# Giving out PSUM by the bank, merging a pair of PE pieces, loading B ahead of x, and planning the kernel's order anew

## The chip, the cores and the metric

One core of one Trainium2 chip. The metric is the device time of one execution in microseconds (us). Every execution has a state: most agree well, some run at a lower granted TensorE clock and are called slow; only fast runs are compared. A "ratio" below is the mean time of one kernel's fast runs over the mean of the other's fast runs in the same rounds on the same chip, with a 95% interval; so it is not quite the ratio of the medians that are quoted beside it.

Medians and ranges in the tables and texts are those of all runs, slow ones included.

Engines: PE is TensorE (PEld its weight loads), DVE VectorE, ACT ScalarE, POOL GpSimd, SP SyncE; SPq and POOLq are the transfers that these issue. PSUM is the memory into which PE's matmuls write; the program uses eight banks of it, of 512 fp32 columns each. "L1105" is line 1105 of the kernel's source. The change moves lines: L1105 (output matmuls) becomes L1110, L1114 (DVE's read of an output) L1119, L877 (B products) L882, L891 (odd states) L889, L741 (stage 1) L747, L754 (spectrum) L760, L780 (inverse) L786, L799 (final) L805, L515 (PSUM copy) L520, L706 (POOL's add on ssm_k) L712, L959 (gates) L964.

## The reference, cut to what matters

```python
# x: 1 x 2048 x 1024, 1024 states, bf16
g = sigmoid((x * gate_w).sum(-1, keepdims=True))
# a: a diagonal state-space model: products with B, a scan over time, products with C
Bu = einsum("bld,pd->blp", x, B_bar)            # complex
h_t = Lam_bar * h_{t-1} + Bu_t
a = 2 * einsum("blp,dp->bld", hseq, C).real + x * Dskip
# b: a long convolution per channel, by Fourier transforms
kv = shift(k, shift_k) * v
b = x * (irfft(rfft(kv) * rfft(ssm_k)) + kv * ssm_D)
out = g * a + (1 - g) * b
```

## The kernel before: the parts that matter

The kernel does not issue its work in program order. It records operations with a duration, a priority and the tiles they use; a planner of its own then simulates the five engines and the buffers, picks a place for each tile, and emits all operations in the order of their planned start. From that order a recording layer underneath derives every semaphore wait. The planner's duties thus include PSUM:

```python
    psums = [psum.tile([128, 1024], F32, name=f"ps{i}") for i in range(4)]   # four allocations of two banks
    ...
    # in the planner: a PSUM tile takes one whole pair of banks, the one that has been free longest
    fr = [i for i in range(self.nps) if psf[i] is None]
    if not fr:
        break
    t.place = min(fr, key=lambda i: self.ps_last[i])
    psf[t.place] = t
```

The last stage makes 32 output tiles of 128x512, each by 16 matmuls and one DVE operation that reads PSUM. Two share one pair of banks:

```python
            ps = pl.psum([2, 512])
            def one(ti):
                def f():
                    for i, pi in enumerate(korder):
                        for ri in range(2):
                            PE_.matmul(ps.ap[:, ti, :], lhsT=Hr[...], rhs=CT[...], start=..., stop=...)
                op("PE", 16 * MM(512), f, r=[...], w=[(ps, ti)], prio=prs[ti])
                op("DVE", 0.77, lambda: STT(out=ot.ap[:, ti, :], in0=ps.ap[:, ti, :], scalar=col(gcols, gi[ti]),
                                            in1=pb.ap[:, ti, :], op0=ALU.mult, op1=ALU.add),
                   r=[(ps, ti), pb, e_gate], w=[(ot, ti)], prio=prs[ti])
            one(0)
            one(1)
```

The states of even steps need products with x (L877) and with the odd states (L891), which before are two PE operations on one PSUM tile. The convolution's kernel ssm_k comes in eight loads of 512 KB; the first is issued by POOL at 8.5 us, beside the first loads of B and x.

## Time and profile before

| | before |
|---|---|
| time, median (lowest to highest), 3 runs | 439.74 us (432.97 to 446.48) |
| profiled run: span, PE busy, DVE busy | 432.5 us, 93%, 80% |

Two groups of the profile before, with PE's output matmuls and DVE's read of them (columns: engine, operation, output and inputs, shapes, count; busy us, mean ns of one; idle us of the engine just before, and what ended it):

```profile
L1105 PE MATMUL ps<-slab,slab 128*128 128x512 bf16 x499 | 111.6, 379 | 2.9 <-DVE slab L1114 1.9
...
L1114 DVE SCALAR_TENSOR_TENSOR slab<-ps,gcols,slab 128x512 bf16<-128x512 f32 x32 | 23.4, 747 | 47.7 <-PE ps L1105 46.1
```

All 32 output tiles together cost PE 2.9 us of idle time. PE hardly ever waits for DVE here.

### The profile page before, as it was taken

Reading aid. Unit: us, or ns where it says so; the run is one execution under the profiler, and the core shown is the slowest. Engines: PE = TensorE matmul, PEld = TensorE weight load, DVE = VectorE, ACT = ScalarE, POOL = GpSimd, SP = SyncE. Lnnn points to the kernel's source line nnn. Section 1 sums busy time; section 2 is a strip of 40 time slices with the busy share of each in tenths; the row PEclk is TensorE's granted clock in tenths of the full one; section 3 lists DMA queues with packets and bytes.
Section 4 is the critical chain, followed back from the end, with each engine's and each line's share of the span. In section 5 each row is a group of like instructions: output and inputs, shape, how many; then the busy total and the mean of one; then the engine's idle time right before and its main releaser. Section 6 shows DMA issues by size and latency. Waiting matters only on the chain. (4 is left out here: it accounts for less than half of the span.)

```text
span 432.5 us, 7209 instructions
## 1 busy us (share of the span) xinstructions
PE 401.3 (93%) x2679; PEld 230.1 (53%) x2726; DVE 344.8 (80%) x509; ACT 282.0 (65%) x316; POOL 144.1 (33%) x190
## 2 busy tenths in 40 slices
PE   7398999999999899999999997998999989999996
PEld 7344545555467555555665654675555534444442
DVE  5974899999999889999999897996767667841542
ACT  3776676599788978986987897895636627211100
POOL 8920763135253565331374562222231200000000
PEclk9979999999999999999999999999999999999999
DMA  9999859946999999999739999997999834611411
GB/s 148 83 190 196 167 120 225 235 106 124 229 246 197 162 179 183 165 156 238 148 71 223 199 182 228 312 243 124 163 206 236 212 72 121 212 56 49 147 36 61
DMA packets 137531, 71.86 MB, mean 166 GB/s; under 512 B 113669, under 2 KB 130325, under 8 KB 137497
## 3 DMA queue, kind: packets, MB, share of 16 engines
q1 hardware_dynamic: 128328, 49.30, 61.8%
q0 software_dynamic: 9088, 22.10, 24.0%
q8 instruction: 21, 0.34, 0.4%
q14 instruction: 14, 0.11, 0.1%
q10 hardware_dynamic: 80, 0.01, 0.0%
HBM read 24.93 MB, written 16.79 MB: 96 GB/s over the span
## 5 line engine op out<-in xcount | busy, mean ns | idle before, releaser
L515 ACT CAST slab<-ps 128x1024 bf16<-128x1024 f32 x194 | 183.0, 1036 | 58.9 <-PE ps L782 13.9
L877 PE MATMUL ps<-slab,slab 128*128 128x512 bf16 (+1 forms) x529 | 115.3, 370 | 8.9 <-DMA slab<-in_A_B_re_dram 6.1
L1105 PE MATMUL ps<-slab,slab 128*128 128x512 bf16 x499 | 111.6, 379 | 2.9 <-DVE slab L1114 1.9
L877 PEld LDWEIGHTS <-slab 128*128 128x128 bf16 x544 | 53.1, 99 | 63.6 <-DMA slab<-in_A_B_re_dram 6.0
L510 POOL DMA_DIRECT2D slab<-slab x92 | 55.7, 611 | 87.7 <-ACT slab L515 78.7
L1105 PEld LDWEIGHTS <-slab 128*128 128x128 bf16 x512 | 49.8, 98 | 60.7 <-issue 2.6
L1114 DVE SCALAR_TENSOR_TENSOR slab<-ps,gcols,slab 128x512 bf16<-128x512 f32 x32 | 23.4, 747 | 47.7 <-PE ps L1105 46.1
L1087 ACT ACTIVATE slab<-slab,omgc 128x512 bf16<-128x512 bf16 x32 | 20.9, 718 | 40.9 <-DMA slab<-pB_scr 40.9
L754 PE MATMUL ps<-slab,fC 128*128 128x512 bf16 x115 | 43.5, 379 | 1.7 <-ACT slab L515 1.1
L906 DVE TENSOR_TENSOR slab<-slab,slab 128x2048 bf16<-128x2048 bf16 x29 | 35.4, 1221 | 7.3 <-ACT slab L515 5.3
L766 DVE TENSOR_TENSOR slab<-slab 128x2048 bf16<-128x2048 bf16 x32 | 38.4, 1215 | 1.2 <-ACT slab L515 1.2
L741 PE MATMUL ps<-tab,slab 128*128 128x128 bf16 x512 | 35.0, 220 | 4.0 <-ACT slab L515 4.0
L741 PEld LDWEIGHTS <-slab 128*128 128x128 bf16 x512 | 31.2, 98 | 8.6 <-issue 5.3
L755 PE MATMUL ps<-slab,fS 128*128 128x256 bf16 x128 | 34.8, 272 | 0.7
L756 PE MATMUL ps<-slab,fN 128*128 128x256 bf16 x128 | 34.9, 272 | 0.0
L780 PE MATMUL ps<-slab,gC 128*128 128x256 bf16 x128 | 29.9, 273 | 2.9 <-DVE slab L770 2.8
L782 PE MATMUL ps<-slab,gS 128*128 128x128 bf16 x128 | 28.0, 219 | 0.0
L781 PE MATMUL ps<-slab,gN 128*128 128x128 bf16 x128 | 28.0, 219 | 0.0
L729 DVE TENSOR_TENSOR slab<-slab,slab 128x2046 bf16<-128x2046 bf16 (+2 forms) x22 | 26.8, 1216 | 0.1
L770 DVE TENSOR_TENSOR slab<-slab 128x512 bf16<-128x512 bf16 x64 | 24.4, 417 | 0.5 <-PE ps L782 0.4
L727 ACT ACTIVATE slab<-slab,skc 128x2047 bf16<-128x2047 bf16 (+2 forms) x11 | 22.2, 2030 | 2.9 <-DMA slab<-in_B_k_dram 2.9
L802 DVE TENSOR_TENSOR slab<-ps,slab 128x1024 bf16<-128x1024 f32 x16 | 19.4, 1220 | 5.0 <-PE ps L800 4.2
(180 smaller groups left out, 553.7 us busy)
## 6 DMA issues: line engine op xcount, KB each, us to landing
slab<-slab POOLq DMA_DIRECT2D x92, 64.0 KB, 6.3
slab<-in_A_x_dram SPq DMA_DIRECT2D x20, 256.0 KB
slab<-kv_scr POOLq DMA_DIRECT2D x8, 512.0 KB, 7.4
slab<-pB_scr SPq DMA_DIRECT2D x16, 256.0 KB
slab<-h_scr SPq DMA_DIRECT2D x8, 512.0 KB
out_dram<-slab SPq DMA_DIRECT2D x15, 256.0 KB
slab<-in_A_x_dram POOLq DMA_DIRECT2D x11, 256.0 KB, 6.4
slab<-in_B_ssm_k_dram SPq DMA_DIRECT2D x5, 512.0 KB
```

Source lines behind the costliest of these rows:

```text
L510: QS[q].dma_start(out=o_, in_=i_)
L515: op("ACT", 1.04, lambda: A.copy(o_(), i_()), r=r, w=w, prio=prio, alt=("DVE", 1.2, lambda: V.tensor_copy(o_(), i_())))
L741: PE_.matmul(ps.ap[:, i, :], lhsT=a.ap[:, 8 * q + i, :], rhs=t1v[:, hh * 128:(hh + 1) * 128], start=True, stop=True)
L754: PE_.matmul(ps.ap[:, i], lhsT=fC[:, k2, :], rhs=zz, start=True, stop=False)
L755: PE_.matmul(ps.ap[:, i, :, 0, :], lhsT=fS[:, k2, :], rhs=zz[:, :, 1, :], start=False, stop=False)
L756: PE_.matmul(ps.ap[:, i, :, 1, :], lhsT=fN[:, k2, :], rhs=zz[:, :, 0, :], start=False, stop=True)
L766: TT(out=T.ap, in0=K.unsqueeze(2).to_broadcast([128, 2, 2, 4 * CH]), in1=W_.unsqueeze(1).to_broadcast([128, 2, 2, 4 * CH]), op=ALU.mult)
L780: PE_.matmul(ps.ap[:, i], lhsT=gC[:, k2, :], rhs=pp.ap[:, :, i, :], start=True, stop=False)
L781: PE_.matmul(ps.ap[:, i, 0, :], lhsT=gN[:, k2, :], rhs=pp.ap[:, 1, i, :], start=False, stop=False)
L877: PE_.matmul(ps.ap[:, ri, k0:k1], lhsT=BT.ap[:, d, ri, :], rhs=t.ap[:, d, k0:k1], start=(d == 0), stop=(par == 1 and d == ND - 1))
L906: TT(out=out, in0=tab.ap.unsqueeze(2).to_broadcast([128, 2, 2, CW]), in1=x.unsqueeze(1).to_broadcast([128, 2, 2, CW]), op=ALU.mult)
L1105: PE_.matmul(ps.ap[:, ti, :], lhsT=Hr[pi, a // 4].ap[:, par, ri, (a % 4) * 128:(a % 4 + 1) * 128], rhs=CT[pi, dh][0].ap[:, CT[pi, dh][1], ...
```

## The change

Intent: a 512-column output needs only one bank, so a bank is to come free as soon as its own tile is read; the even-state tile is to be held for a shorter time; the loads that PE needs first are to be alone on the DMA engines; and the planner's priorities and buffer counts were searched anew for this. Cut to its core (new priorities left out: they change every number of the tables):

```diff
     def psum(self, shape):
+        t.banks = 1 if n <= 512 else 2
...
-                    fr = [i for i in range(self.nps) if psf[i] is None]
+                    n = t.banks
+                    fr = [i for i in range(0, self.nps, n) if all(x is None for x in psf[i:i + n])]
-                    t.place = min(fr, key=lambda i: self.ps_last[i])
-                    psf[t.place] = t
+                    t.place = min(fr, key=lambda i: (n == 1 and psf[i ^ 1] is None, max(self.ps_last[i:i + n])))
+                    psf[t.place:t.place + n] = [t] * n
...
-                        a = psums[t.place]
+                        a = psums[t.place // 2][:, 512 * (t.place % 2):]
...
-    NSLAB, NPS = 21, 4
+    NSLAB, NPS = 21, 8
...
         def load_A(src, u, tag, ex, pr):
+            ex = ex + ([(xT[0, NC - 1], 1)] if u < 2 else [])     # not before the last x tile
...
-            (even states: part(0, CW) and the odd-state products as two PE operations)
+                op("PE", 2 * ND * MM(CW) + 4 * MM(511) + (0.2 if c else 0), lambda: (part(0, CW), prev()), ...)
...
-        BTs = [loadB(0, (-1000, -988.5)), loadB(1, (-986.5, -986))]
+        BTs = [loadB(0, (-1000, -999)), loadB(1, (-986.5, -986))]
...
-            ps = pl.psum([2, 512])
             def one(ti):
+                ps = pl.psum([512])
-                            PE_.matmul(ps.ap[:, ti, :], ...
+                            PE_.matmul(ps.ap, ...
```

## The prediction

> **What bounds the kernel now.** I read the page first (parts 1 and 2), then busy time by stretches, then PE's waits, then the instructions in order of time around each wait.
>
> ```profile
> span 432.5 us, 7209 instructions
> PE 401.3 (93%) x2679; PEld 230.1 (53%) x2726; DVE 344.8 (80%) x509; ACT 282.0 (65%) x316; POOL 144.1 (33%) x190
> ...
> PE   7398999999999899999999997998999989999996
> ...
> PEclk9979999999999999999999999999999999999999
> ```
>
> PE is the bound: 93% busy, and the thin slices lie at the start, about two thirds on, and around 355 us. No change of the diff removes a matmul, so the question is how much of the span is not needed by PE. I work PE's own need out from rows where it runs without a gap: the chain has 49 output matmuls of 512 columns (L1105) in 10.74 us, 0.219 us each. L1105 512, the B products L877 512 (in whole equivalents), L891 and L943/L945 64+32+64, L799/L800 64: 1248 x 0.219 = 273.6 us. The spectrum (L754 to L756) takes 0.435 us a step, x128 = 55.7; the inverse (L780 to L782) 0.89 us a piece of four steps, x32 = 28.5; stage 1 (L741) 0.45 us a piece, x64 = 28.6; gates and small ones some 3.5. Sum 390 us. So 432.5 - 390 = 42.5 us are lost, and only these can be won.
>
> ```profile
> 15.00:20.00 5.00, 1.42 (x14) 1.02 (x11) 4.85 (x20) 4.97 (x3) 4.91 (x4) 0.95 1.00 57
> 20.00:25.00 5.00, 2.43 (x6) 1.04 (x8) 4.82 (x8) 3.31 (x10) 3.88 (x4) 0.50 1.21 194
> ...
> 265.00:270.00 5.00, 2.22 (x13) 1.14 (x13) 2.31 (x3) 4.80 (x6) 1.28 (x5) 0.87 1.04 284
> ```
>
> The columns are PE, PEld, DVE, ACT, POOL busy, clock, DMA share, GB/s. Up to 46.3 us PE does only about 24.4 us of the needed work (96 B products 21.0, gates 2.0, the rest 1.4): **head loss 21.9 us**. After the last matmul (428.5 us) come 4.0 us of last DVE operation and store: **tail loss 4.0**. The rest, **16.6 us, is lost in the body**.
>
> ```profile
> 11.07 1.91 PE L877 MATMUL ps<-slab,slab 128*128 128x256 bf16 x16
> 14.52 1.91 PE L877 MATMUL ps<-slab,slab 128*128 128x256 bf16 x16 [1.54 <-DMA slab<-in_A_x_dram]
> 22.57 15.69 PE L877 MATMUL ps<-slab,slab 128*128 128x512 bf16 x78 [6.15 <-DMA slab<-in_A_B_re_dram]
> ```
>
> The largest single gap is 6.15 us at 22.57: PE has used x's first tile for state block 0 and waits for B of block 1. After it the clock is 0.50 until 26.4 us, another 1.9 us lost.
>
> ```profile
> PE ps L741 <- ACT slab L515: 4.0, 6, 2.7
> PE ps L780 <- DVE slab L770: 2.8, 3, 1.5
> PE ps L1105 <- DVE slab L1114: 1.9, 1, 1.9
> PE ps L754 <- ACT slab L515: 1.1, 4, 0.3
> ```
>
> (Total, times, longest.) Stage 1 reads only loaded data and constants, so its wait on ACT's PSUM copy is a wait for a free PSUM pair. With the same kind at L754, L943, L877, L891 and L1105, waits for a pair or for what was just copied come to some 7.4 us in the body; L780's are for DVE's product and no PSUM matter.
>
> **What the Trainium skill says.** "TensorE: Matmul & The Clock Gate", Part 1: an idle window of about 3.4 us brings the clock to half, and as much busy time restores it. The trace agrees: after the 6.15 us gap the clock is 0.50. At 267 us a gap of 2.67 us also cost clock (0.87), so shorter gaps are not safe. "DMA: Bandwidth & Descriptors", Issuing engines are not separate DMA queues: transfers from different engines interleave on the same 16 DMA engines. The trace agrees: the POOL queue issues a 512 KB load of ssm_k at 8.52 us, and B's 512 KB, issued at 8.91 and 10.26, land only at about 22.2, in a stretch that runs down to 57 GB/s. "PSUM — Partial Sum Buffer", the four PSUM rules: one matmul output is at most one bank, 512 fp32 columns. So a 512-column output tile needs just one bank; giving it two is the plan's grain, not the chip's need.
>
> **The change part by part.**
>
> *x before the convolution's loads, B ahead of x.* Loads of ssm_k and kv for the first two channel blocks, and the first x rows of the convolution, now wait for the last transposed x tile. B_im of block 0 moves ahead of x, but the first 16 matmuls need both B halves and the first x piece anyway, so that order is worth about 0. Taking ssm_k away is worth more. x's second half tile lands at 14.5. From 22.2 to 40.9 the six other x half tiles come at 18.7 / 6 = 3.1 us per 512 KB. At that rate B of block 1 lands at 14.5 + 3.1 = 17.6, say 18, not 22.2, and the last x at 36.7, not 40.9. PE and DVE both wait for x in the head (gates at 40.96, the first rotations after it), so the plan starts some **4.2 us earlier**; the gap shrinks to about 2 us and most of the 1.9 us of cold clock goes, though part of that only becomes waiting for x: **-0.5**. Moved to later: the 512 KB of ssm_k. Its first user, stage 1, is at 38.1 us, so it may now be late; PE has other blocks' B products then, so I take 0.
>
> *PSUM per bank.* Only the 32 output tiles (and the gates) are one bank; spectrum, stage 1, inverse, final and B products still take an aligned pair. So up to 291 us, where L1105 starts, it changes next to nothing. After it, an output pair was held until both halves had been read. Here is what that cost:
>
> ```profile
> 352.29 0.75 DVE L1114 SCALAR_TENSOR_TENSOR slab<-ps,gcols,slab 128x512 bf16<-128x512 f32 x1 [3.44 <-PE ps L1105]
> 355.07 0.75 DVE L1114 SCALAR_TENSOR_TENSOR slab<-ps,gcols,slab 128x512 bf16<-128x512 f32 x1
> 355.87 6.42 PE L1105 MATMUL ps<-slab,slab 128*128 128x512 bf16 x29 [1.90 <-DVE slab L1114]
> ```
>
> PE sat 1.90 us until DVE had read the second half at 355.07, since the other pairs held two final pieces. With banks the first half is free at 353: **-1.9**, and -0.3 for the wait at 291. From 362 to 428 outputs run without a gap already: nothing to win there.
>
> *Even products in one piece.* Before, a pair was taken at the x part and kept until the odd states were there: at 231.65 the x part ends, at 236.5 the four L891 start, 4.9 us with three pairs left for all else; elsewhere 0 to 3 us. 16 such pieces. No instruction is saved. The small waits of 0.2 to 0.5 us for a pair, in all about 4.4 us without the one of 2.67, have other causes too (ACT needs 1.02 us for a pair, a conv piece on PE 0.45 to 0.89), so I give this a quarter: **-1.1**.
>
> *Priorities and buffer counts.* This moves everything and removes nothing. What is left of the body's loss after the above is 16.6 - 3.3 = 13.3 us, among it 4.2 us around 267 (a 2.67 us wait and the clock after it): ACT stood behind a pB read that came late, which a plan does not foresee. A newly searched order may win some of that and meet new late transfers: **-1.5, give or take 4**.
>
> Sum: -4.2 - 0.5 - 2.2 - 1.1 - 1.5 = -9.5, span 423.0. The profiled run took 434.26 us for a span of 432.5, so 1.8 more: 424.8 in a quiet run. The three timed runs were 432.97, 439.74 and 446.48; the quiet one lies 1.3 below the profiled run and the middle one 5.5 above. I take 2 us of such scatter: **427 us**.
>
> **Rivals.** (a) *DVE becomes the bound of the body.* From 46 to 290 us DVE is busy 229.5 of 244 us (94%), PE 232.9 (95%). If the chain of rotations and scans on DVE sets when the outputs may start, a faster PE start is won only as far as DVE starts sooner too, and PSUM relief is worth nothing. For: DVE is at 4.9 to 5.0 of 5 us in most stretches. Against: DVE drops to 3.2 of 10 us from 30 to 40 while it waits for the first states, which come earlier too; and from 290 on it has room for convolution work. It would make -5 us: 430 quiet. (b) *The new plan runs into late transfers.* Loads put off in the head make ssm_k or kv late for stage 1, and ACT or PE, strictly in order, stand behind them, as at 267. Each such event costs 3 to 4 us with the clock; two of them leave 429 to 432. (c) *False ordering between two banks of one tile*: an output in one bank would wait for the reader of its neighbour. Against: before, PE wrote the second half while DVE read the first, without a gap for 66 us. Would cost 10 us or more; I give it 3%. (d) *The search does better*: DVE work moved behind 300 us, body loss halved, head as computed: -14, 418.5 quiet.
>
> **Range and chances.** Main path and its neighbours 423 to 429, (a) and (b) up to 434, (d) down to 418; scatter of some us: 418 to 436. The quiet run of before is 433 to 434, so 2% faster means below about 425, just where my quiet estimate lies; measured against the median before, 427 is 2.9% faster. Hence 0.54 faster, 0.43 within 2%, 0.03 slower.
>
> **What would show it.** Right: in the changed kernel PE's gap before block 1's B products is at most 3 us and ends by 19, the clock stays near 1.00 there, gates start by 37.5; no wait of L1105 on L1114 over 0.5 us; the L891 matmuls follow straight on their L877; PE busy falls only by 1 to 3 us, nearly all of the gain being idle time. Wrong: ssm_k was not what delayed B (the gap stays 5 us or more); PE's waits on the PSUM copy stay at 6 us or more; or new waits on transfers over 2 us between 50 and 360 us.

## The result, and the profile after

| | before | after |
|---|---|---|
| median (lowest to highest) of 6 runs each | 439.39 us (432.97 to 446.48) | 458.06 us (454.64 to 467.53) |
| ratio, fast runs | | 1.046, interval 1.034 to 1.058 |
| profiled run, both fast | 434.26 us | 457.16 us |

The change is 4.6% slower. Parts 1 and 2 of the page after (in the rows of part 2 each digit stands for a fortieth of the span and gives the busy share, or the granted clock, in tenths):

```profile
span 455.4 us, 7234 instructions
...
PE 405.7 (89%) x2679; PEld 231.4 (51%) x2726; DVE 346.6 (76%) x511; ACT 289.2 (64%) x315; POOL 148.0 (33%) x192
...
PE   7789999999899998999899887899699988787875
...
PEclk9999999999999999999999999899799999999999
```

The work is the same; PE is 89% busy and not 93%. Compare the ends of the two PE rows. Before, the last seven slices were 9s but for the final one; after, they are 8, 7, 8, 7, 8, 7, 5: PE loses a fifth of its time in the very stage that had nothing to lose. The first digits are better than before, and the clock in the head no longer drops. Stretches of the head after (columns as in the prediction):

```profile
15.00:20.00 5.00, 3.46 (x19) 1.77 (x20) 4.85 (x20) 4.54 (x3) 4.92 (x4) 1.00 1.10 210
20.00:25.00 5.00, 4.12 (x28) 2.41 (x26) 4.44 (x8) 4.08 (x10) 4.83 (x3) 1.00 1.08 180
```

PE in order of time in the head, after:

```profile
16.54 5.15 PE L882 MATMUL ps<-slab,slab 128*128 128x512 bf16 x31 [1.54 <-DMA slab<-in_A_B_re_dram]
...
22.57 8.87 PE L882 MATMUL ps<-slab,slab 128*128 128x512 bf16 x47 [0.88 <-DMA slab<-in_A_x_dram]
...
35.19 1.91 PE L964 MATMUL ps<-slab,gwb 128*32 128x512 bf16 x31 [2.57 <-DMA slab<-in_A_x_dram]
```

The 6.15 us wait for B is 1.54 us, and the bulk of the gates starts at 35.2, not 40.96. The head came out as meant. PE's waits (us in total, times, longest):

```profile
PE ps L1110 <- DVE slab L1119: 18.8, 21, 1.9
...
PE ps L747 <- POOL slab L712: 2.6, 1, 2.6
PE ps L786 <- ACT slab L520: 2.3, 4, 1.1
...
PE ps L747 <- ACT slab L520: 1.4, 4, 0.7
```

The first line is new: 21 times PE, about to start an output tile, waited for DVE's read of an output. The same in the groups of the page:

```profile
L1110 PE MATMUL ps<-slab,slab 128*128 128x512 bf16 x485 | 115.5, 386 | 19.5 <-DVE slab L1119 18.8
...
L1119 DVE SCALAR_TENSOR_TENSOR slab<-ps,gcols,slab 128x512 bf16<-128x512 f32 x32 | 23.8, 749 | 72.3 <-PE ps L1110 71.3
```

DVE's read is as long as before (749 ns), and DVE is idle 72 us ahead of these reads, so DVE is not overloaded: it waits for PE, and PE for it. How, shows in order of time, first PE, then DVE:

```profile
367.13 3.61 PE L1110 MATMUL ps<-slab,slab 128*128 128x512 bf16 x16 [0.84 <-DVE slab L1119]
371.58 3.61 PE L1110 MATMUL ps<-slab,slab 128*128 128x512 bf16 x16 [0.84 <-DVE slab L1119]
376.04 3.61 PE L1110 MATMUL ps<-slab,slab 128*128 128x512 bf16 x15 [0.84 <-DVE slab L1119]
```

```profile
370.78 0.75 DVE L1119 SCALAR_TENSOR_TENSOR slab<-ps,gcols,slab 128x512 bf16<-128x512 f32 x1 [1.78 <-PE ps L1110]
375.24 0.75 DVE L1119 SCALAR_TENSOR_TENSOR slab<-ps,gcols,slab 128x512 bf16<-128x512 f32 x1 [3.71 <-PE ps L1110]
```

A strict turn: a tile on PE (367.13 to 370.74), then DVE's read (370.78 to 371.53), then the next tile (371.58). One tile takes 4.45 us where its matmuls need 16 x 0.219 = 3.50 us. With eight banks to choose from, an output's matmuls and an output's read never run at the same time here.

The list of the built program's instructions, with their places and waits, says why (counts are those that each engine's semaphore has reached):

```
after                                             before
MM tile 30 -> ps1, bank 0   waits DVE 508         MM tile 25 -> ps1, bank 1   waits DVE 493
   ends: PE count 2710                            MM tile 26 -> ps1, bank 0   waits for nothing
   DVE reads tile 29, ps1 bank 1, waits PE 2710      ends: PE count 2646
   done: DVE count 509                               DVE reads tile 25, ps1 bank 1, waits PE 2646
MM tile 31 -> ps1, bank 1   waits DVE 509            DVE reads tile 26, ps1 bank 0
   ends: PE count 2726                            MM tile 27 -> ps3, bank 1   waits DVE 496
```

After: tile 29 is complete before tile 30 starts, but its reader waits for PE count 2710, the **end of tile 30, which goes to the other bank**. That wait is not needed by the data. Tile 31 then truly has to wait for this reader, as it gets tile 29's bank. So each read falls between two tiles. The wait exists because the recording layer orders by the whole allocation `ps1` of two banks. In the program before, the same unneeded wait is there (tile 25 is read only after the end of tile 26), but PE's next tile goes to another allocation and does not feel it. The new key sends outputs into the half next to a taken half, so from one point on all outputs alternate between the two banks of `ps1`.

To see where else time came and went, I followed PE's progress: each matmul's weight load counted with the duration that the prediction's rows give it, so that the total is 390 us. The table has the time at which a given amount of this work was begun, minus the same of before's profiled run (-5 is 5 us ahead). It depends on the durations taken, most of all at 105, and is to be read to some 2 us. It is used for all runs below.

| needed work begun (us) | 30 | 105 | 240 | 255 | 300 | 330 | end |
|---|---|---|---|---|---|---|---|
| after | -5.1 | -7.3 | -7.9 | -1.1 | +4.4 | +5.4 | +22.4 |
| e2_spread | -4.6 | -6.8 | -1.4 | +7.1 | +5.7 | +4.9 | +4.9 |
| e6_earlyk | -1.3 | -3.5 | -4.9 | +2.5 | +1.1 | +0.3 | +0.3 |
| e7_lastk | -5.2 | -7.4 | -8.6 | -2.3 | -3.8 | -3.8 | -3.8 |
| e9_lastk5 (same kernel as e7) | -4.5 | -6.7 | -8.1 | +2.6 | +0.5 | -1.5 | -1.5 |
| e5_latek (slow) | -2.4 | +3.1 | +6.9 | +6.9 | +8.1 | +8.1 | +8.1 |

After is 5 to 8 us ahead until 240, gives all of it and 4 us more back between 240 and 300, and loses another 17 us in the outputs. Each row is a single run, and before's profiled run (434.26 us) was one of its quicker ones, so differences of some 5 us at the end are within scatter.

### The profile page after: what moved, and what is told of

It reads as the page before. It is cut to its first block, busy times and chain, and to the rows that moved or that the text cites. A ratio compares the mean times of both kernels' runs of the same rounds, so it can differ in the third digit from the quotient of the medians.

```text
span 455.4 us, 7234 instructions
## 1 busy us (share of the span) xinstructions
PE 405.7 (89%) x2679; PEld 231.4 (51%) x2726; DVE 346.6 (76%) x511; ACT 289.2 (64%) x315; POOL 148.0 (33%) x192
## 3 DMA queue, kind: packets, MB, share of 16 engines
q0 software_dynamic: 9456, 23.41, 22.4%
## 4 chain that ended last, share of the span: by engine, by line
PE 59%; DVE 12%; DMA 7%; issue 7%; SPq 7%; POOL 3%; ACT 3%; DVEq 0%; POOLq 0%; ACTq 0%
PE ps L1110 23%; PE ps L882 17%; SPq L513 6%; DMA slab<-slab 6%; DVE slab L1119 4%; PE ps L747 3%; POOL slab L515 2%; ACT slab L520 2%; PE ps L760 2%; PE ps L889 2%; PE ps L786 2%; DVE slab L520 2%; PE ps L950 2%; DMA slab<-in_A_x_dram 2%; DVE slab L772 2%
## 5 line engine op out<-in xcount | busy, mean ns | idle before, releaser
L520 ACT CAST slab<-ps 128x1024 bf16<-128x1024 f32 x188 | 178.1, 1037 | 49.8 <-PE ps L788 16.6
L1110 PE MATMUL ps<-slab,slab 128*128 128x512 bf16 x485 | 115.5, 386 | 19.5 <-DVE slab L1119 18.8
L882 PE MATMUL ps<-slab,slab 128*128 128x512 bf16 (+1 forms) x529 | 113.9, 366 | 4.2 <-DMA slab<-in_A_B_re_dram 1.5
L1119 DVE SCALAR_TENSOR_TENSOR slab<-ps,gcols,slab 128x512 bf16<-128x512 f32 x32 | 23.8, 749 | 72.3 <-PE ps L1110 71.3
L760 PE MATMUL ps<-slab,fC 128*128 128x512 bf16 x113 | 42.8, 379 | 3.4 <-DVE slab L808 1.5
L747 PE MATMUL ps<-tab,slab 128*128 128x128 bf16 x512 | 35.4, 225 | 4.1 <-POOL slab L712 2.6
L733 ACT ACTIVATE slab<-slab,skc 128x2047 bf16<-128x2047 bf16 (+2 forms) x18 | 36.2, 2019 | 1.7 <-DVE slab L735 1.0
L747 PEld LDWEIGHTS <-slab 128*128 128x128 bf16 x512 | 32.2, 101 | 7.6 <-POOL slab L712 2.8
L786 PE MATMUL ps<-slab,gC 128*128 128x256 bf16 x128 | 29.9, 272 | 3.8 <-ACT slab L520 2.3
L735 DVE TENSOR_TENSOR slab<-slab,slab 128x2047 bf16<-128x2047 bf16 (+2 forms) x24 | 29.2, 1216 | 0.1
L520 DVE CAST slab<-ps 128x1024 bf16<-128x1024 f32 x20 | 24.2, 1216 | 6.1 <-PE ps L747 5.9
```

What stands on the lines that cost most here:

```text
L520: op("ACT", 1.04, lambda: A.copy(o_(), i_()), r=r, w=w, prio=prio, alt=("DVE", 1.2, lambda: V.tensor_copy(o_(), i_())))
L733: alt=("ACT", 2.05, lambda: A.activation(out=tmp.ap[:, 0:n], in_=kT.ap[:, 0:n], func=ACT.Copy, scale=skc[:, u, j:j + 1])))
L747: PE_.matmul(ps.ap[:, i, :], lhsT=a.ap[:, 8 * q + i, :], rhs=t1v[:, hh * 128:(hh + 1) * 128], start=True, stop=True)
L760: PE_.matmul(ps.ap[:, i], lhsT=fC[:, k2, :], rhs=zz, start=True, stop=False)
L786: PE_.matmul(ps.ap[:, i], lhsT=gC[:, k2, :], rhs=pp.ap[:, :, i, :], start=True, stop=False)
L882: PE_.matmul(ps.ap[:, ri, k0:k1], lhsT=BT.ap[:, d, ri, :], rhs=t.ap[:, d, k0:k1], start=(d == 0), stop=(par == 1 and d == ND - 1))
```

## The experiments

Theory: the 4.6% is the false order (a wait that the data do not need) between two banks of one allocation, met by a placement that uses only two banks. Rivals: the new plan's order is slower in itself; the head's change; or the chip cannot write a bank while its neighbour is read. The parts cannot be undone one by one simply: each undoing makes the planner replan, and with priorities searched for something else it plans badly (see e11_oldplan). So most runs keep the changed kernel's order on every engine, which was compared instruction by instruction, and change one thing.

**e1_turn: same order, outputs in turn through all four allocations.** After planning, output tiles that start later than the last two-bank tile get their banks in a fixed turn:

```diff
     order = pl.schedule(...)
+    last = max(o.end for o in order for t in o.tiles if t.size == 0 and t.banks == 2) + 0.5
+    turn = (0, 2, 4, 6, 1, 3, 5, 7)
+    seen = []
+    for o in order:
+        for t in o.tiles:
+            if t.size == 0 and t.banks == 1 and o.start > last and t not in seen and o.eng == "PE":
+                t.place = turn[len(seen) % len(turn)]
+                seen.append(t)
```

> The changed kernel with the same order of instructions on every engine; only the PSUM banks of the output tiles that start after the last two-bank tile are given out anew, each tile in another two-bank allocation than the tile before. Theory (false ordering): the reader of one bank waits for the writer of the other bank of the same allocation, and with two banks in turn the next tile then waits for that reader, 0.84 us a tile. Some 20 tiles are concerned: about 17 us less than the changed kernel, near 438 to 441 us, PE's waits on the output's DVE operation down from 18.8 to about 2 to 3 us. Rival (DVE itself is too late or too slow in this plan, or the new plan is bad): no change, 455 to 459 us.

**e2_spread: same order, the placement key turned round.** A one-bank tile prefers an allocation of which nothing is taken:

```diff
-  (n == 1 and psf[i ^ 1] is None, max(self.ps_last[i:i + n]))
+  (n == 1 and psf[i ^ 1] is not None, max(self.ps_last[i & -2:(i & -2) + 2]))
```

> The changed kernel with the same order on every engine; the rule that prefers a bank whose neighbour is taken is turned round, so that every output tile, also those between convolution pieces, prefers an allocation that nobody uses. False-ordering theory: as the turned one and besides the 1.94 us wait at 325 us with its cold clock goes: 434 to 438 us, output waits below 1 us in all. If what remains over the kernel before is the new plan's own, it lands within 3 us of the kernel before on either side. Rival: no change, 455 to 459.

**e3_pairs: as e1_turn, but both banks of an allocation one after the other.** The turn is (0, 1, 2, 3, 4, 5, 6, 7): the false wait stays, but a bank is reused only eight tiles later.

```diff
-    turn = (0, 2, 4, 6, 1, 3, 5, 7)
+    turn = (0, 1, 2, 3, 4, 5, 6, 7)
```

> As the turned one, but consecutive tiles take banks 0,1,2,...,7: two neighbours share an allocation, the third moves on. The reader of tile n still waits for the writer of tile n+1 for every second n, but PE never needs that bank next. Theory (it takes both, the false wait and the reuse of only two banks): same time as the turned one within 1.5 us, DVE's output operations in groups of two late by 3.5 us. Rival (the neighbouring bank alone costs, by the chip or by a wait of the writer): half of the 17 us stay, some 8 us slower than the turned one.

**e4_nobanks: the PSUM part undone, all else of the change kept** (its planner's order differs from the change's in a few places on PE, DVE, ACT and POOL, so it is nearly, not wholly, the same).

```diff
-    NSLAB, NPS = 21, 8
+    NSLAB, NPS = 21, 4          # and the planner's lines on banks as in the kernel before
-                ps = pl.psum([512])
+            ps = pl.psum([2, 512])
```

> The changed kernel with the PSUM part undone: two-bank tiles given out in turn over four allocations, the outputs in pairs; all else of the change, priorities too. The planner's order differs in few places. Theory: the waits of 0.84 us are gone, 434 to 440 us. If the priorities or the head were to blame for the loss, it stays at 450 or more.

Measured, all four beside runs of the kernel before (436.18 us median of 7):

| | median (lowest to highest), 4 runs | ratio to before | output matmuls waiting for L1119 (before's L1114) |
|---|---|---|---|
| after (from its own call) | 458.06 | 1.046 | 18.8 us, 21 times |
| e1_turn | 443.20 us (436.71 to 450.26) | 1.003, 0.994 to 1.013 | 2.8 us, twice |
| e2_spread | 436.87 us (435.63 to 438.84) | 1.001, 0.995 to 1.008 | none |
| e3_pairs | 440.98 us (439.04 to 446.56) | 1.010, 1.000 to 1.020 | 2.8 us, twice |
| e4_nobanks | 445.61 us (439.36 to 450.02) | 1.009, 1.000 to 1.019 | 3.6 us, once (slow run) |

PE's waits in e1_turn that matter (total, times, longest), and the output group of e2_spread:

```profile
PE ps L747 <- POOL slab L712: 5.5, 1, 5.5
PE ps L1110 <- DVE slab L1119: 2.8, 2, 1.9
```

```profile
L1110 PE MATMUL ps<-slab,slab 128*128 128x512 bf16 x485 | 109.6, 379 | 1.2 <-DVE slab L808 0.6
```

With not one instruction moved, the idle time before output matmuls falls from 19.5 to 1.2 us in e2_spread, and the time from 458 to 437 us. So the placement of the outputs is the whole of the slowdown, within the interval of e2_spread. e3_pairs tells which half of the mechanism costs: the false wait alone costs PE next to nothing (2.8 us are left, as in e1_turn, from two early tiles); it needs the reuse of just two banks. The fast runs of e3_pairs are 2.4 us above those of e1_turn (440.3 against 437.9 us), more than the 1.5 us foretold and far less than the 8 us of the rival; the intervals overlap, and PE's output waits are the same. And the rest of the change, without its fault, is at 1.001 and not at the 0.971 (427 / 439.74) that I predicted: nothing of my 9.5 us arrived. e4_nobanks is not told apart from e2_spread by these intervals; half of its runs were slow, its profiled one too, and its fast runs (439.36 and 441.89) end at or above the 434 to 440 us foretold.

**e8_banks: the chip or the bookkeeping?** A kernel of its own, with wrong results: sections of 16 output tiles, alike but for how two banks are given out.

```diff
+ pair  = psum.tile([128, 1024])            # L42: two banks of one allocation, in turn
+ bank0 = psum.tile([128, 512])             # L46: two neighbouring banks, two allocations, in turn
+ bank1 = psum.tile([128, 512])
+ pair2 = psum.tile([128, 1024])            # L50: as L42, each read listed before the next tile's matmuls
+ # L63: control, in turn through the halves of two allocations
```

> Wrong results on purpose: the output stage alone, four sections of 16 tiles, each tile 16 matmuls of 128x512 into one PSUM bank, then one VectorE read of 128x512. Section 1 turns over two allocations of two banks (warm-up and control); section 2 alternates between the two banks of one allocation, as the changed kernel does; section 3 alternates between two neighbouring banks that are two allocations; section 4 is section 2 with each read listed in the program before the next tile's matmuls. Theory (the order is made by the program's bookkeeping of whole allocations, the chip can write one bank while the neighbour is read): 3.5 us a tile without a gap in sections 1 and 3, 4.3 to 4.5 us a tile with a gap of 0.8 us in 2 and 4. Rival (neighbouring banks themselves cannot be written and read at the same time): section 3 has the gap too, or its matmuls or reads are longer by 0.3 us a tile or more.

The groups of e8_banks, PE's and then DVE's (L66, L56, L59 and L53 read the tiles of L63, L46, L50 and L42):

```profile
L63 PE MATMUL pair<-xa 128*128 128x512 bf16 x251 | 58.0, 393 | 3.7 <-DMA xa<-in_A_x_dram 3.4
L50 PE MATMUL pair<-xa 128*128 128x512 bf16 x251 | 57.4, 379 | 13.1 <-DVE ob L59 12.9
L42 PE MATMUL pair<-xa 128*128 128x512 bf16 x251 | 57.2, 379 | 12.2 <-DVE ob L53 12.0
L46 PE MATMUL bank<-xa 128*128 128x512 bf16 x251 | 55.2, 379 | 0.3
...
L56 DVE SCALAR_TENSOR_TENSOR ob<-bank,one,xa 128x512 bf16<-128x512 f32 x16 | 12.0, 751 | 42.6 <-PE bank L46 42.6
...
L53 DVE SCALAR_TENSOR_TENSOR ob<-pair,one,xa 128x512 bf16<-128x512 f32 x16 | 11.9, 750 | 58.0 <-PE pair L42 54.3 <-remote 3.7
```

Two neighbouring banks that are separate allocations: 0.3 us idle, 16 tiles in one unbroken stretch of 55.42 us, 3.46 us a tile. The control, L63, has no gap but the 3.4 us for its first load. The same two-bank turn within one allocation: gaps of 0.84 us, in order of time a tile every 4.46 us, as in the changed kernel. The read takes 751 ns beside matmuls into the neighbour and 750 ns alone. So in this run, the only one of e8, the chip works on neighbouring banks at once without cost, and the order was made by the bookkeeping. The Trainium skill, "PSUM — Partial Sum Buffer", The four PSUM rules, says "Each bank is a separate physical SRAM"; this run agrees. Section 4 shows that listing the read earlier does not help: then the next tile's matmuls wait for the read of the other bank.

**e5_latek: the head part alone, on the kernel before.** Its first ssm_k load is issued from POOL after x's loads; order elsewhere kept.

```diff
+    k0 = pl.tags["ka"][0]
+    mv = [o for o in order if k0 in o.tiles and o.eng != "PE"]
+    rest = [o for o in order if o not in mv]
+    at = next(i for i, o in enumerate(rest) if o.start > 26.0)
+    order = rest[:at] + mv + rest[at:]
```

> The kernel before with one edit: its first load of ssm_k (512 KB) is issued from GpSimd after x's loads (planned at 26 us) and not at 8.5 us; the order on every other engine is as before. It does the head part of the change alone. If the step of my prediction is right, that B and x share the transfers with ssm_k, the PE wait of 6.1 us for B at 22.6 us falls to 1 to 3 us and PE is 3 to 5 us ahead when 30 us of its needed work are done. Theory 'given back': the rest of the plan starts nothing earlier, so at the end less than 2 us are left of it (ratio 0.995 to 1.0). Rival 'kept': the ratio is 0.990 (4 us). If the wait stays at 5 us or more, the load was not what slowed B.

**e6_earlyk: the head part undone alone, in e2_spread.** The first ssm_k load goes back to the front of POOL's order.

```diff
+    k0 = pl.tags["ka"][0]
+    mv = [o for o in order if k0 in o.tiles and o.dma is not None]
+    rest = [o for o in order if o not in mv]
+    at = next(i for i, o in enumerate(rest) if o.eng == "POOL" and o.start > 8.0 and o.dma is None)
+    order = rest[:at] + mv + rest[at:]
```

> The mirror of the run before: the changed kernel with its banks spread (e2_spread, 437 us), with the first ssm_k load issued from GpSimd early, at some 8 us, as in the kernel before. The head part of the change undone alone. Expected: PE waits 5 us or more for B and x again, and is 3 to 5 us behind e2_spread at 30 us of work. Theory 'given back': the end is within 2 us of e2_spread's (ratio to before 1.00 to 1.006). Rival 'kept': 4 to 5 us later (ratio 1.01).

PE in the head, e5_latek and then e6_earlyk:

```profile
18.80 12.25 PE L877 MATMUL ps<-slab,slab 128*128 128x512 bf16 x63 [4.01 <-DMA slab<-in_A_B_re_dram]
```

```profile
23.44 14.50 PE L882 MATMUL ps<-slab,slab 128*128 128x512 bf16 x71 [5.97 <-DMA slab<-in_A_B_im_dram]
```

Measured: e5_latek 440.34 us (434.88 to 442.35, 4 runs), ratio 1.005 (0.990 to 1.020); e6_earlyk 436.03 us (431.69 to 439.88), ratio 1.000 (0.983 to 1.017); before there 438.47 us, 7 runs. In e6_earlyk the wait of 6 us is back, and the start is 3.3 us later than e2_spread's (-1.3 against -4.6 in the table): the ssm_k load does slow B. In e5_latek the wait fell only to 4.0 us, not to the 1 to 3 I expected, and PE was only 2.4 us ahead at 30. The lead at 30 varies between runs of one program, though: e3_pairs, with the late load, waited 3.0 us for B and 3.4 us for x and was about 1 us ahead in its profiled run. The wait for B tells more: 6.15 and 5.97 us in the two traces with the early load (before, e6_earlyk), 0.3 to 3.0 us with the late one in every fast trace of the new plan. But neither moved the end: with the head's gain undone the kernel is not slower, and with the head's gain given to the kernel before it is not faster. So "given back" is what these runs favour over "kept", which would have been 4 us in each; the intervals are wide enough for 4 us to hide in either alone. e5's profiled run was slow, and its row is not used for more than its head.

**e7_lastk and e9_lastk5: one late load repaired.** In the profiled runs of the new plan up to e6_earlyk PE waits at some 285 to 292 us for POOL's add on the last ssm_k load. SP issues it; SP's order of time in e2_spread, and PE's wait:

```profile
274.99 2.09 SPq L513 DMA_TRANSPOSE slab<-in_A_C_im_dram  x1
277.19 0.52 SPq L515 DMA_DIRECT2D slab<-in_A_x_dram  x1
277.80 4.39 SPq L515 DMA_DIRECT2D slab<-in_B_ssm_k_dram  x1
```

```profile
PE ps L747 <- POOL slab L712: 3.7, 1, 3.7
```

The load stands behind four transposing loads of C, which themselves waited for buffers, and lands near 292 us. The edit gives it to POOL as soon as its buffer is free:

```diff
+    k7 = pl.tags["ka"][-1]
+    o = next(o for o in order if k7 in o.tiles and o.dma is not None)
+    order.remove(o)
+    o.eng, o.fn = "POOL", o.alt[2]
+    order.insert(next(i for i, x in enumerate(order) if x.start > 273.4), o)
```

> The changed kernel with its banks spread, and its last load of ssm_k issued by GpSimd as soon as its buffer is free (planned 273 us) instead of by SyncE behind four transposing loads (issued at 277.8, landed near 292 us in e2_spread, where PE waited 3.7 us for it). If late loads are where the gain of the head goes, the PE wait for the GpSimd add falls under 0.5 us and the time is 2 to 4 us under e2_spread (433 to 435 us, ratio to before 0.99 to 0.996). If another wait takes its place at once, the time stays at 436 to 438.

> The kernel of e7_lastk again, with five rounds: e7's ratio 0.9966 left an interval from 0.984 to 1.009. Theory: with the false order gone and the last ssm_k load early, some 3 us of the head's gain reach the end, as e7's trace showed (3.8 us ahead of before at the end): ratio 0.990 to 0.997. Rival: e7's profiled run was a lucky one, and the ratio is 1.00 to 1.005 as for e2_spread.

**e10_ctlate: two of those transposing loads moved behind x's load as well**, into a stretch in which SP issued nothing.

```diff
+    late = [o for o in order if o.dma is not None and 262 < o.start < 265 and o.tiles[0].tag == "CT"]
+    order = [o for o in order if o not in late]
+    at = next(i for i, x in enumerate(order) if x.start > 279.0)
+    order[at:at] = late
```

> e7_lastk with two of the four transposing loads of C that SyncE issues between 254 and 272 us moved behind x's load, into a stretch of 6.5 us in which SyncE had nothing to issue. In e7 PE waited 2.8 us at 270.4 for a transfer that ran beside those four. If they were what delayed it, that wait falls under 1 us and the time is 1 to 3 us under e9 (ratio 0.985 to 0.995). If not, the same wait stays and the ratio is e9's.

Measured: e7_lastk 434.77 us (430.25 to 439.50, 4 runs), ratio 0.997 (0.984 to 1.009); e9_lastk5 433.61 us (430.63 to 436.85, 6 runs), ratio **0.988 (0.981 to 0.996)**; e10_ctlate 434.46 us (431.53 to 437.07, 6 runs), ratio 0.990 (0.983 to 0.996); before beside the last two 439.81 us, 11 runs. The wait for L712 is gone in e7 and e9, and e9's interval lies under 1. It is 1.2%, about half of the 2.2% that the predicted 9.5 us are, and within the 2% that counts as the same. Not all of it need be the kernel's: before's fast runs took 438.9 us on average, at a granted clock of 0.975 to 0.988, against 435.4 us at 0.984 to 0.992 in e1 to e4 on the same chip. e9's ran at 0.991 to 0.998 and took 433.5 us, e7's, the same kernel, 433.3 us. Against 435.4 us that is 0.4%. Whether this version keeps the clock up by having fewer gaps, or before only met worse runs, is not shown. e9's trace shows what still eats the head's lead. PE, and then ACT:

```profile
271.49 0.38 PE L805 MATMUL ps<-slab,tabFc 128*128 128x512 bf16 x1 [3.34 <-DMA slab<-in_A_C_re_dram]
...
286.92 0.59 PE L760 MATMUL ps<-slab,fC 128*128 128x512 bf16 x1 [3.94 <-ACT slab L520]
```

```profile
284.82 1.15 ACT L1038 ACTIVATE slab<-slab,cco 128x1024 bf16<-128x1024 bf16 x1 [4.12 <-DMA slab<-in_A_C_im_dram]
```

ACT, strictly in order, stood 4.12 us behind a late load of C, and PE 3.94 us behind the PSUM copy that ACT had next. PE's two waits, 3.34 and 3.94 us, are 7.3 of the 10.7 us that e9 loses between the columns 240 and 255. e10_ctlate moved two of those loads and gained nothing over e9: in its trace PE waits 3.8 us at L805 for transfers and 3.1 us at L760 for DVE instead. The late transfers change places; one move does not remove them.

**e11_oldplan: e2_spread's parts with the priorities and caps (buffer counts) of the kernel before.**

```diff
-    PS, PU, PO, PC, PH, PG, PX, CAPS, SPARE, NBIG = (those of the change)
+    PS, PU, PO, PC, PH, PG, PX, CAPS, SPARE, NBIG = (those of the kernel before)
```

> All structural parts of the change with spread banks, but with the priorities and caps of the kernel before: is the redone plan a gain of its own, or only what the other parts need? The planner's own sum for this order is 468 us, against 431 with the new priorities. Theory 'needed': 460 us or more. Rival 'the new numbers are worth a few microseconds at most': under 445.

One run: 463.92 us (state unknown), against 439.81 of before. PE's longest waits:

```profile
PE ps L805 <- DMA slab<-slab: 6.9, 1, 6.9
PE ps L948 <- ACT slab L520: 6.2, 4, 5.4
```

With the old numbers the same parts cost 24 us in this one run, so the structural parts need the redone plan. Whether new numbers alone would gain anything on the kernel before, no run tests.

## Why the prediction was wrong

Predicted: 427 us, range 418 to 436, 0.03 for slower. Measured: 458.06, slower. By its own steps:

**The step that failed is in "PSUM per bank": rival (c) was set aside**, "an output in one bank would wait for the reader of its neighbour", 10 us or more, 3%. It happened, with 18.8 us, in a form slightly other than named: the reader waited for the neighbour's writer, and the next output for that reader. My evidence against it was "PE wrote the second half while DVE read the first, without a gap for 66 us". I had read only PE's side of that: PE had no gap. I never looked at when DVE read. In before's trace, matched with the program's list, none of the 32 reads runs while PE works on the other bank of its allocation. One line of DVE's order of time would have raised the doubt:

```profile
400.96 2.07 DVE L1114 SCALAR_TENSOR_TENSOR slab<-ps,gcols,slab 128x512 bf16<-128x512 f32 x3 [10.49 <-PE ps L1105]
```

DVE waited 10.49 us for PE and then read three tiles at once, while PE finishes one every 3.5 us. By the list, the first of these reads is of tile 22, in bank 1 of `ps3`, and it waits for the end of tile 23, in bank 0 of `ps3`, 3.5 us after tile 22 was complete. The other two, of tiles 20 and 21, stood behind it in DVE's order. The false order was in the kernel before; four allocations in turn hid it from PE. The prediction also missed the second half of the mechanism, which stood in the diff: a key that packs one-bank tiles into a half-used pair.

**PSUM per bank, -2.2.** Came with the opposite sign. The 1.90 us wait at 355.87 for a pair is gone, and 21 waits of together 18.8 us took its place. In e2_spread, with the banks well placed, the outputs wait 1.2 us in all instead of 2.9, so the step may have been right in kind, 1.7 us of 2.2, once the placement was repaired; the new plan also differs there, and no run separates the two.

**Head, -4.2 - 0.5.** The mechanism was right by all three of its tests: the gap before block 1's B products was 1.54 us (at most 3 foretold) and over by 16.5 (19), the clock there 1.00, the bulk of the gates at 35.2 (37.5). PE was 5 us ahead at 30 and 8 at 240. What failed is the next thought, that such a lead reaches the end. Rival (b), late transfers, took it back between 240 and 255 us of work, where e7 and e9 show the loads by name (7.3 of 10.7 us in e9; for the changed kernel itself the sum is not worked out). In the profiled runs of e7 and e9 3.8 and 1.5 us of the lead reach the end.

**Even products in one piece, -1.1.** The odd-state matmuls follow straight on, as foretold. PE's waits for PSUM copies did not fall: some 9 us in the body after, against 7.7 before counted alike. The prediction had named 6 us or more as a sign of being wrong. L741's 4.0 became 1.4 at L747, but L786 and L805, which waited 0.3 us at most for ACT before, now wait 2.3 and 1.9. No run did this part alone, so its own worth stays open.

**Plan, -1.5 give or take 4.** e2_spread at 1.001 contains it together with the head and the merge, so it cannot be read alone. e11_oldplan, one run, has 24 us lost without it, far more than 4: I had treated as an optional gain what the other parts need. PE's busy time rose by 4.4 us (405.7 against 401.3), where a fall of 1 to 3 was foretold.

**DVE as bound, rival (a).** Not seen, but not tested by a run of its own. DVE was as busy in the body (226.2 of the 244 us from 46 to 290, against 229.5 before), and yet the lead held until 240 us of work; in e7 PE reached 94% with the same DVE work.

**A slip.** Rival (d)'s "418.5 quiet" is a span; with the 1.8 us that the prediction adds elsewhere it would be a run of 420.3 us. Nothing hangs on it.

What stays open: how much of the head's lead a plan could keep at best, how much of e9's 1.2% over the kernel before is the kernel's own and not the clock's, and whether it would hold against another search of the old plan.

## What to carry to other kernels

Before splitting a buffer into finer parts, find out at which grain the waits are derived: a part of an allocation may be free by the data and still be ordered by the whole. Read both sides of a hand-over in the trace, since an engine without gaps says nothing about a reader that comes late; and place consecutive tiles in different allocations. A lead in the head of a strictly ordered plan is only worth what the late loads further on leave of it.

## What the Trainium skill lacked or had wrong

- "PSUM — Partial Sum Buffer" says that banks are separate memories, and that holds (751 ns a read beside matmuls into the neighbour, 750 without). It lacks, as do the other pages, that a program's waits may be derived per allocation, so that two banks of one allocation behave as one: 4.46 us a tile against 3.46 for the same work.
- "TensorE: Matmul & The Clock Gate", Part 1, gives an idle window of about 3.4 us for the clock to halve; neither it nor the rest of the page gives a length of shorter idle stretches that do so. In the changed kernel two gaps of 1.51 and 1.94 us, ending at 321.88 and 324.88 us with work between them, came with a clock of 0.50 from 324.0 to 330.9 us; gaps of 0.84 us in every 4.46 us did not lower it (1.00 from 362 to 453 us).
